# First modulation weights on ScalarE's queue, a fixed order of the first loads, new planning costs and new seeds in an attention-plus-MLP block

## The chip, the cores and the metric

The kernel runs on one core of one Trainium2 chip. The metric is the device time of one execution in microseconds (us), the median of three runs. Durations of single instructions come from one profiled execution.

## What is computed

One transformer block with adaptive layer norm, batch 1, 2048 positions, width 512, 32 heads of 16, hidden width 1376, all in bf16:

```python
mod = (_silu(c) @ w_mod).reshape(c.shape[0], 6, 1, -1)
sa, ca, ga, sb, cb, gb = (mod[:, 0], ..., mod[:, 5])
h = _layernorm(x) * (1 + ca) + sa
x = x + ga * _A_ref(h, A_wqkv, A_wo)         # attention: softmax(q k^T / 4) v, then @ wo
h = _layernorm(x) * (1 + cb) + sb
x = x + gb * _B_ref(h, B_w1, B_b1, B_w2, B_b2)   # gelu(h @ w1 + b1) @ w2 + b2
```

## The kernel before, in words

**Runs and tiles.** The 2048 positions form four blocks of 512 queries. A run is one block of queries with four heads; there are 32 runs, each over 16 tiles of 128 keys. One tile of one run is four score matrices of 128x512, one per head, called units here: 32 x 16 x 4 = 2048 units in all. TensorE multiplies the scores (L853), four heads at a time on four row groups of the array.

**Two engines make the exponentials.** ScalarE takes most units: TensorE writes three or two of them into one of two PSUM tiles `st` (three and two banks wide, in turn), and one ACTIVATE (L926) makes `pt` of them. The other units go to VectorE: TensorE writes one into a PSUM bank `ax`, VectorE turns it into an integer phase `ph` (L967), and then, once for four units, makes shifted copies `sh` (L987), four per tile, of which some fourth copies are made by GpSimd in four pieces `sg` (L1003). Reinterpreted as bf16, each copy is a coarse exponential, and the four together, weighted in the values `VX`, give a fine one. TensorE multiplies the results with the values into `od` (L1038). So an ScalarE tile costs one set of products, a VectorE tile four.

**What sets the order.** Every instruction stream is written out by hand from a planner (`Plan`) that runs while the program is built. It keeps a list of ready operations per engine, each with a planned duration and a priority; it commits the earliest, and breaks near ties with a pseudo-random term (`spread`) drawn from `SEEDS`, one seed for each 16 us of planned time. Planned durations decide which unit goes to which engine and where on TensorE's stream each product stands: `A_US` for ScalarE's ACTIVATEs of one, two or three units, `POOL_US` and `G_US` for GpSimd's pieces, `kb` for a load's landing (planned bytes over a planned rate). The engines then run these fixed streams; only semaphores decide the real times. Where the planner sees too little recent work on TensorE, it puts in filler products with a tile of zeros (`warm`): L463 and L468 before the first run, L479 (`zeros`, four products on `od`) beside a product set later.

**The start.** SyncE's queue issues, in this order: the first block of `x` in two halves (`xb`, L534), the first two 512-column parts of `w_mod` (1 MB into `g`, L544), the first 128 columns of the three projection weights (`w`, L551), the second block of `x` (L524), the other columns of the weights. ScalarE's queue issues `c` alone (L518). The modulation vectors are 32 narrow products with `g` (L611), copied by VectorE (L624, L625). The normalised block `z` is turned by TensorE (L687, 16 products), then scaled and shifted by the modulation on VectorE (L654, two quarters) and ScalarE (L651, two quarters) into `blk`; from `blk` come the first keys and queries (L730), and then the first scores.

**Late work.** After the first run, the remaining weights are loaded, some behind memsets on GpSimd that zero their padding (L1151 to L1153); after run 24 the last rows of `wo` are spread over a tile `wop` behind a memset (L1178). In each block's MLP a memset puts a row of ones into `g` (L1232), which brings in the bias. An operation of kind "beside" on GpSimd is planned beside a VectorE instruction, and waits for the VectorE instruction before that one (`after_dve`). After the last run come its division, the projection, the layer norm and the MLP of the last 256 positions, on TensorE almost without a break.

Of the kernel before, what the change touches and what calls it, by code (L numbers as in the profile page):

```python
# [11 lines left out]
ACT = mybir.ActivationFunctionType  # L12
# [51 lines left out]
FILL = 2.1  # L64
HOLD = 0.0
SPREAD = 0.15
SEEDS = (29, 932, 256, 388, 841, 336, 949, 269, 862, 134, 634, 182, 632, 486, 660, 374, 610, 152, 531, 667, 387, 332, 696, 744, 409, 494, 133, 981, 473, 660, 675, 515, 555, 629, 58, 269, 671, 382, 338, 452, 367, 48, 574, 712, 716, 126, 732, 265, 528, 970)
HEAT = 1.7


# [211 lines left out]
def kernel(  # L282
# [14 lines left out]
    nc = tc.nc  # L297
# [18 lines left out]
    FEW = 1  # L316
    MM = 0.2155
    SPAN = (3, 2)
    POOL_US, POOL_MIN = 0.68, 0.5
    G_US, G_MIN, G_PRIO, G_MAX, G_FROM, G_TILES = 0.70, 0.5, 1.0, 4, 60.0, 6  # L320
    A_US = {1: 0.477, 2: 0.904, 3: 1.3305}
    AHEAD = 3
    FIRST_DKS, D_TIME = (14,), 8.0

# [208 lines left out]
    for h in range(2):  # L533
        o_x0 += 2 * [dma(lambda o, h=h: nc.sync.dma_start(out=o_x[0].tile[:, 2 * h:2 * h + 2, :],  # L534
                                                         in_=x_src[0][:, 2 * h:2 * h + 2, :]),
                         (o_x[0],), kb=256, prio=0.0)]
    g0 = op("NIL", None, 0.0, (), lat=0.0, prio=-2.0, acq=r_g)

    def mod_pair(tile_):
# [1 line left out]

    def mod_part(tile_, n):
        return mod_pair(tile_)[:, :, n * D:(n + 1) * D]
    o_wm = dma(lambda o: nc.sync.dma_start(out=mod_pair(g0.tile), in_=wm_src[:, :, 0:2 * D]), (g0,), kb=1024, prio=0.01)  # L544
    o_w, o_w0 = {}, {}
    for i in range(3):
        o_w[i] = op("NIL", None, 0.0, (), lat=0.0, prio=-1.0 + 0.1 * i, acq=r_w)
# [1 line left out]
    def load_cols(i, lo, hi, prio):  # L549
        def go(o):  # L550
            nc.sync.dma_start(out=o_w[i].tile[:, :, lo:hi], in_=wq_src[:, :, i * D + lo:i * D + hi])  # L551
        return dma(go, (o_w[i],), kb=(hi - lo) * (2 if lo == 0 else 1), prio=prio, n=2.7)
    o_w0 = {i: load_cols(i, 0, P, 0.1 + 0.01 * i) for i in range(3)}
    o_w1 = {}
    for b in range(1, NQ):
        o_x[b] = load_x(b)
        o_x[b].prio = 0.2 + 0.1 * b
        o_w1[b - 1] = load_cols((1, 2, 0)[b - 1], P, D, 0.25 + 0.1 * b)
    o_w1 = {i: o_w1[(1, 2, 0).index(i)] for i in range(3)}

    o_id = op("POOL", lambda o: make_identity(nc, ident), 0.5, prio=0.0)
# [499 lines left out]
    def normalise(r):  # L1061
        last, od = o_last[r], o_od[r]
        OD = op("DVE", lambda o: nc.vector.tensor_copy(out=o.tile, in_=od.tile), 0.6, (last,),  # L1063
                prio=0.0, acq=r_OD, rel=(od,))
        st = {}

        def d1(o):
            st["dn"] = drp.tile([4, QB], FP32, name="dn")
            nc.sync.dma_start(out=st["dn"], in_=OD.tile[16:P:32, :])
        o1 = dma(d1, (OD,), kb=8, prio=0.0)  # L1070
        o2 = dma(lambda o: nc.sync.dma_start(
            out=o.tile, in_=st["dn"].rearrange("i (s e) -> (i s) e", e=16)), (o1,), kb=8, prio=0.0,
            acq=r_dc)
# [16 lines left out]
        two = beside(lambda c: nc.gpsimd.tensor_tensor(  # L1090
            out=OT.tile[:, c], in0=OD.tile[:, c], in1=o5.tile[:, c], op=ALU.mult), (OT,), (OD, o5), free=r == NR - 2)
        if not move:
            OT.two = two
            o_OT[(b, u // 2)] = OT
            return
        to = OT if b == LAST else o_OT[(b, u // 2)]

        def shift(o):
            for i in range(4):
                nc.sync.dma_start(out=to.tile[32 * i + 16:32 * i + 32, 0:HB] if b == LAST else  # L1100
                                  to.tile[32 * i + 16:32 * i + 32, :],
                                  in_=OT.tile[32 * i:32 * i + 16, HB:QB] if b == LAST else
                                  OT.tile[32 * i:32 * i + 16, :])
# [14 lines left out]
        return scaled([lambda f=f: W2[f // 4].tile[:, f % 4, :] if f < 8 else W2c[:, f - 8, :] for f in range(NF)],  # L1118
                      gb_bc, (W2[0], W2[1], o_late["small"], o_late["gb"]))

    def beside(fn, deps, rel=(), prio=0.5, free=False):

        if free:
            return [op("POOL", lambda o, c=c: fn(slice(c * HB, (c + 1) * HB)), POOL_US, deps, lat=0.1, prio=0.1,
                       rel=rel, port=True) for c in range(2)]
        return [op("POOL", lambda o, c=c: after_dve(fn(slice(c * HB, (c + 1) * HB))), POOL_US, deps, lat=0.1,
                   prio=prio, kind="beside", rel=rel, port=True, gate=lambda: plan.beside(POOL_MIN))
                for c in range(2)]

# [10 lines left out]
    def late_loads(after):  # L1140
# [7 lines left out]
        def wo(o):  # L1148
# [1 line left out]
        o_late["wo"] = dma(wo, d, kb=512)  # L1150
        z2 = op("POOL", lambda o: (nc.gpsimd.memset(W1[:, :, F:NF * P], 0.0),  # L1151
                                   nc.gpsimd.memset(b1_bf, 0.0),
                                   nc.gpsimd.memset(W2c[:, 2, :], 0.0)), 1.5, d, prio=8.0)  # L1153
        o_late["w1"] = dma(lambda o: nc.sync.dma_start(
            out=W1[:, :, 0:F], in_=B_w1.rearrange("(j p) n -> p j n", p=P)), (z2,), kb=1400)

# [13 lines left out]
    def split_wo():  # L1170
        held["wop"] = wop = op("NIL", None, 0.0, (), lat=0.0, prio=0.0, acq=r_w)

        def load(o):
            wo_src = A_wo[(NC - 1) * P:NC * P, :].rearrange("(r p d) f -> r p d f", r=4, p=2)
            for r in range(4):
                for p in range(2):
                    nc.sync.dma_start(out=wop.tile[32 * r:32 * r + 16, p, :], in_=wo_src[r, p])
        z1 = op("POOL", lambda o: nc.gpsimd.memset(wop.tile[:, 0:2, :], 0.0), 0.9, (wop,), prio=1.0)  # L1178
        ld = dma(load, (z1,), kb=128, n=8, prio=3.0)
        o_late["wop"] = scaled([lambda p=p: wop.tile[:, p, :] for p in range(2)], ga_bc, (ld,))  # L1180

    def fold_w1():
# [46 lines left out]
        return P if f < NF - 1 else FL  # L1229

    def ones(g, deps):
        return op("POOL", lambda o: nc.gpsimd.memset(g.tile[FL:P, NF - 1, :], 1.0), 0.4, deps, prio=0.0)  # L1232

    def finished():
        return units[0] == NR * NT * 4
# [317 lines left out]
```

## Time and profile before

| what | value |
|---|---|
| median of 3 runs (lowest to highest) | 775.24 us (774.72 to 776.56) |
| the profiled execution's own time | 774.01 us |
| span of its trace | 772.1 us |
| TensorE, VectorE, ScalarE, GpSimd busy | 94%, 93%, 96%, 43% of the span |
| granted TensorE clock | 0.998 |

A group of instructions is told by line, engine, operation, output and input tile; a busy time counts overlapping instructions once, a mean is that of single instructions. In the timeline a row gives the start, the length of a merged stretch of equal instructions, and their number; a bracket names the idle time ahead of it and what ended that. Consecutive instructions of one engine overlap, so their distance from start to start is shorter than their duration.

### The profile page before, as it was taken

The page shows a single profiled execution, that of the slowest core. Times are in us where ns is not written, and L with a number is a line of the kernel's source. Part 1 is how long each engine was busy: PE and PEld are TensorE (multiplying, and loading weights), DVE is VectorE, ACT ScalarE, POOL GpSimd, SP SyncE. Part 2 cuts the span into 40 slices and gives each one's busy share as a digit, 9 for nine tenths or more (in the row PEclk, how much of TensorE's full clock was granted, in tenths as well). Part 3 has the DMA queues.
Part 4 walks back from the last instruction along what each step waited for, and adds up shares of the span by engine and source line. Part 5 has one row for each costly group of instructions (what it writes and reads, how often), then busy time and mean ns, then how long its engine had stood idle before and what let it go on. Part 6 is the DMA issues. An engine that isn't in the chain of part 4 may idle for free. (4 is left out here: it accounts for less than half of the span.)

```text
span 772.1 us, 20489 instructions
## 1 busy us (share of the span) xinstructions
PE 726.5 (94%) x8066; PEld 263.9 (34%) x8066; DVE 718.5 (93%) x1233; ACT 744.8 (96%) x673; POOL 333.9 (43%) x604
## 2 busy tenths in 40 slices
PE   9999999999999989989999999999999899999997
PEld 4433333333332322222322222222233334433445
DVE  6889799889999999999999999999989999999984
ACT  4999999999999999999999999999999999999993
POOL 6512533555554454545541353434434544341441
PEclk9999999999999999999999999999999999999999
DMA  6151010100011001011110120001111111101100
GB/s 219 34 156 64 18 51 17 26 3 19 24 53 44 23 25 45 20 31 25 44 30 26 31 35 20 22 21 28 33 47 27 29 32 33 46 19 31 33 18 28
DMA packets 42162, 29.53 MB, mean 38 GB/s; under 512 B 25525, under 2 KB 35286, under 8 KB 42066
## 3 DMA queue, kind: packets, MB, share of 16 engines
q1 hardware_dynamic: 42058, 28.22, 13.1%
q8 instruction: 63, 1.03, 0.6%
q14 instruction: 33, 0.27, 0.1%
q10 hardware_dynamic: 8, 0.00, 0.0%
HBM read 20.77 MB, written 2.61 MB: 30 GB/s over the span
## 5 line engine op out<-in xcount | busy, mean ns | idle before, releaser
L926 ACT ACTIVATE pt<-st 128x1536 bf16<-128x1536 f32 (+1 forms) x621 | 704.4, 1350 | 3.7 <-PE ax L853 2.3
L967 DVE TENSOR_SCALAR ph<-ax 128x512 int16<-128x512 f32 x496 | 325.1, 681 | 23.1 <-PE ax L853 20.6
L1003 POOL TENSOR_SCALAR sg<-ph 128x512 int16<-128x512 int16 x320 | 199.8, 624 | 293.3 <-DVE sh L987 186.5
L987 DVE TENSOR_SCALAR sh<-ph 128x2048 int16<-128x2048 int16 x416 | 285.0, 715 | 1.9 <-PE od L1038 1.0
L853 PE MATMUL st<-qm,kT 32*128 32x512 bf16 x1552 | 243.2, 382 | 31.9 <-ACT pt L926 25.6
L853 PE MATMUL ax<-qm,kT 32*128 32x512 bf16 x496 | 170.4, 380 | 3.7 <-DVE ph L967 2.2
L853 PEld LDWEIGHTS <-kT 32*128 32x128 bf16 x2048 | 85.6, 91 | 250.1 <-issue 240.7
L1038 PE MATMUL od<-pt,VEB 128*32 128x512 bf16 (+1 forms) x1936 | 142.3, 341 | 1.5 <-DVE OD L1063 1.0
L1038 PE MATMUL od<-sh,VX 128*32 128x512 bf16 (+1 forms) x1464 | 110.5, 342 | 1.1 <-DVE sh L987 0.7
L1038 PEld LDWEIGHTS <-VEB 128*32 128x32 bf16 x2560 | 61.6, 96 | 75.1 <-issue 60.7
L1038 PEld LDWEIGHTS <-VX 128*32 128x32 bf16 x1872 | 44.4, 95 | 70.5 <-issue 63.3
L1038 PE MATMUL od<-sh,VEB 128*32 128x512 bf16 (+1 forms) x624 | 49.5, 341 | 0.3 <-DVE sh L987 0.2
L1090 POOL TENSOR_TENSOR OT<-OD,RB 128x256 bf16<-128x256 f32 x38 | 27.9, 745 | 43.5 <-DVE sh L987 33.6
L1284 PE MATMUL ax<-blk,W 128*128 128x512 bf16 (+1 forms) x176 | 43.6, 355 | 0.4 <-DVE ph L967 0.4
L479 PE MATMUL od<-warm 128*32 128x512 bf16 x416 | 40.4, 387 | 0.0
L730 PE MATMUL ax<-blk,w 128*128 128x512 bf16 x124 | 35.9, 382 | 0.5 <-ACT blk L651 0.2
L1225 PE MATMUL ax<-w,g 128*128 128x512 bf16 x128 | 34.4, 381 | 0.9 <-ACT g L1294 0.6
L1038 PE MATMUL od<-sg,VX 128*32 128x512 bf16 (+1 forms) x408 | 32.1, 338 | 0.2 <-POOL sg L1003 0.2
L788 POOL TENSOR_SCALAR VX<-VEB 128x128 bf16<-128x128 bf16 x60 | 22.4, 377 | 19.3 <-PE od L1038 10.7
L1289 DVE TENSOR_SCALAR g<-ax,b1c 128x512 bf16<-128x512 f32 (+1 forms) x44 | 29.2, 675 | 1.2 <-PE ax L1284 0.9
L1090 POOL TENSOR_TENSOR OS<-OD,RB 128x256 bf16<-128x256 f32 x24 | 17.1, 728 | 28.0 <-DVE sh L987 27.6
L635 DVE BATCH_NORM_STATS2 ln_s<-xb 128x6 f32<-128x512 bf16 x32 | 21.7, 677 | 1.4 <-DMA xb<-in_A_x_dram 1.4
(107 smaller groups left out, 412.1 us busy)
## 6 DMA issues: line engine op xcount, KB each, us to landing
RB<-rn SPq DMA_DIRECT2D x124, 64.0 KB
xb<-in_A_x_dram SPq DMA_DIRECT2D x7, 512.0 KB
g<-in_w_mod_dram SPq DMA_DIRECT2D x2, 1024.0 KB
out_dram<-o SPq DMA_DIRECT2D x16, 128.0 KB
qm<-qs SPq DMA_DIRECT2D x120, 16.0 KB
W<-in_B_w_dram SPq DMA_DIRECT2D x1, 1376.0 KB
w<-in_A_wqkv_dram SPq DMA_DIRECT2D x3, 384.0 KB
xb<-in_w_mod_dram SPq DMA_DIRECT2D x2, 512.0 KB
```

The costliest lines, as they stand in the source:

```text
L479: nc.tensor.matmul(out=o_od[r].tile[32 * i:32 * i + 32, :], lhsT=warm[:, 0:32], rhs=warm[:, 0:1].to_broadcast([P, QB]), start=False, stop= ...
L730: return chain([(lambda ps, j=j: nc.tensor.matmul(out=ps[:, 0:QB], lhsT=w.tile[:, j, cc * P:(cc + 1) * P], rhs=o_h[b].tile[:, j, :], start ...
L853: nc.tensor.matmul(out=o.tile[:, k * QB:(k + 1) * QB], lhsT=kT[cc][kb][rows, ko * P:(ko + 1) * P], rhs=qm.tile[rows, par, :] if hb is None ...
L926: nc.scalar.activation(out=e.tile[:, 0:total * QB], in_=o.tile[:, 0:total * QB], func=ACT.Exp, scale=ESC)
L967: nc.vector.tensor_scalar(out=ph.tile[:, o.row * QB:(o.row + 1) * QB], in0=o.tile, scalar1=PH_B, scalar2=PH_LOW, op0=ALU.add, op1=ALU.max)
L987: nc.vector.tensor_scalar(out=o.tile, in0=first.tile, scalar1=1.0 / FINE, scalar2=PH_0 + PH_SH[j], op0=ALU.mult, op1=ALU.add)
L1003: after_dve(nc.gpsimd.tensor_scalar(out=sh.tile[:, c], in0=first.tile[:, c], scalar1=1.0 / FINE, scalar2=PH_0 + PH_SH[j], op0=ALU.mult, op ...
L1038: nc.tensor.matmul(out=o_od[r].tile[32 * i:32 * i + 32, n * HB:n * HB + w], lhsT=v_tile(kt, ph)[:, c0:c0 + 32], rhs=got[i][:, at:at + w], ...
L1090: two = beside(lambda c: nc.gpsimd.tensor_tensor(out=OT.tile[:, c], in0=OD.tile[:, c], in1=o5.tile[:, c], op=ALU.mult), (OT,), (OD, o5), f ...
L1225: nc.tensor.matmul(out=ps, lhsT=g[:, f, col:col + P], rhs=rhs, start=(f == 0), stop=(f == NF - 1))
L1284: mm = chain([(lambda ps, f=f, j=j, f0=f0: nc.tensor.matmul(out=ps[:, (f - f0) * N:(f - f0 + 1) * N], lhsT=W1[:, j, f * P:(f + 1) * P], rh ...
L1289: ev.append(op("DVE", lambda o, f=f, f0=f0, mm=mm: nc.vector.tensor_scalar(out=g.tile[:, f, 0:N], in0=mm.tile[:, (f - f0) * N:(f - f0 + 1) ...
```

## The change

1. The 1 MB load of the first modulation weights is issued from ScalarE's queue, right behind the load of `c`; its planned size goes from 1024 to 1300 (kB), and the planner makes it depend on the load of `c`.
2. The first loads on SyncE's queue get priorities that fix their order: the halves of `x`, then the first columns of the weights in the order keys, queries, values (before: queries, keys, values), then in turn a block of `x` and the rest of one weight. The planned size of the first columns is halved.
3. Planned durations: ScalarE's ACTIVATEs from 0.477, 0.904, 1.3305 us to 0.487, 0.916, 1.344 us; GpSimd's multiplication of the attention output from 0.68 to 0.74 us; the late memsets from 1.5 to 1.2 and from 0.4 to 0.52 us, with the port that GpSimd shares with VectorE taken into account.
4. The memset of `wop` is cut into four pieces placed "beside" VectorE; the memset of ones is placed so too.
5. All 50 seeds are new.

```diff
-SEEDS = (29, 932, 256, ...)
+SEEDS = (432, 324, 180, ...)
...
-    POOL_US, POOL_MIN = 0.68, 0.5
+    POOL_US, POOL_MIN, N_US = 0.68, 0.5, 0.74
-    A_US = {1: 0.477, 2: 0.904, 3: 1.3305}
+    A_US = {1: 0.487, 2: 0.916, 3: 1.344}
...
-                         (o_x[0],), kb=256, prio=0.0)]
+                         (o_x[0],), kb=256, prio=-9.0 + h)]
...
-    o_wm = dma(lambda o: nc.sync.dma_start(out=mod_pair(g0.tile), in_=wm_src[:, :, 0:2 * D]), (g0,), kb=1024, prio=0.01)
+    o_wm = dma(lambda o: nc.scalar.dma_start(out=mod_pair(g0.tile), in_=wm_src[:, :, 0:2 * D]), (g0, o_c), kb=1300,
+               eng="ACT", prio=-7.0)
...
-        return dma(go, (o_w[i],), kb=(hi - lo) * (2 if lo == 0 else 1), prio=prio, n=2.7)
-    o_w0 = {i: load_cols(i, 0, P, 0.1 + 0.01 * i) for i in range(3)}
+        return dma(go, (o_w[i],), kb=hi - lo, prio=prio, n=2.7)
+    o_w0 = {i: load_cols(i, 0, P, -6.0 + (1, 0, 2)[i]) for i in range(3)}
...
-        o_x[b].prio = 0.2 + 0.1 * b
-        o_w1[b - 1] = load_cols((1, 2, 0)[b - 1], P, D, 0.25 + 0.1 * b)
+        o_x[b].prio = b - 3.5
+        o_w1[b - 1] = load_cols((1, 2, 0)[b - 1], P, D, b - 3.0)
...
-                                   nc.gpsimd.memset(W2c[:, 2, :], 0.0)), 1.5, d, prio=8.0)
+                                   nc.gpsimd.memset(W2c[:, 2, :], 0.0)), 1.2, d, prio=8.0, port=True)
...
-        z1 = op("POOL", lambda o: nc.gpsimd.memset(wop.tile[:, 0:2, :], 0.0), 0.9, (wop,), prio=1.0)
-        ld = dma(load, (z1,), kb=128, n=8, prio=3.0)
+        z1 = [x for p in range(2) for x in beside(
+            lambda c, p=p: nc.gpsimd.memset(wop.tile[:, p, c], 0.0), (wop,), us=0.35)]
+        ld = dma(load, z1, kb=128, n=8, prio=3.0)
...
-        return op("POOL", lambda o: nc.gpsimd.memset(g.tile[FL:P, NF - 1, :], 1.0), 0.4, deps, prio=0.0)
+        return op("POOL", lambda o: after_dve(nc.gpsimd.memset(g.tile[FL:P, NF - 1, :], 1.0)), 0.52, deps, lat=0.1, prio=0.0,
+                  kind="beside", port=True, gate=lambda: plan.beside(POOL_MIN))
```

Since the planner lays out every stream anew, the instruction lists of the two built programs differ beyond these lines. Counted in the two lists:

| instructions | before | after |
|---|---|---|
| ScalarE, ACTIVATE of three units / of two units | 310 / 311 | 310 / 309 |
| VectorE, `ph` / `sh` | 496 / 416 | 500 / 421 |
| GpSimd, `sg` pieces | 320 | 316 |
| TensorE, products with the values, in sets of four | 660 whole, 448 half-width | 663 whole, 448 half-width |
| TensorE, filler sets of four on `od` (L479, and L1029 at a run's start) | 104 + 8 | 121 + 8 |
| TensorE, fillers of full width (L463, L468) | 51 | 47 |
| TensorE, ahead of the narrow products of L611: fillers / products that turn `z` | 29 / 0 | 30 / 8 |

In the lists of the changed kernel the last streams, from the last score product to the end, hold the same instructions as before in a slightly different order.

More of the change, by code (lines that the diff above doesn't have):

```diff
@@ L66 @@
 SPREAD = 0.15
-SEEDS = (29, 932, 256, 388, 841, 336, 949, 269, 862, 134, 634, 182, 632, 486, 660, 374, 610, 152, 531, 667, 387, 332, 696, 744, 409, 494, 133, 981, 473, 660, 675, 515, 555, 629, 58, 269, 671, 382, 338, 452, 367, 48, 574, 712, 716, 126, 732, 265, 528, 970)
+SEEDS = (432, 324, 180, 701, 660, 159, 105, 688, 614, 64, 722, 921, 341, 292, 667, 446, 7, 423, 524, 376, 479, 681, 179, 178, 891, 61, 111, 982, 774, 605, 458, 798, 627, 354, 348, 796, 559, 345, 786, 415, 117, 962, 210, 627, 701, 917, 778, 631, 597, 949)
 HEAT = 1.7
@@ L1090, in normalise @@
         two = beside(lambda c: nc.gpsimd.tensor_tensor(
-            out=OT.tile[:, c], in0=OD.tile[:, c], in1=o5.tile[:, c], op=ALU.mult), (OT,), (OD, o5), free=r == NR - 2)
+            out=OT.tile[:, c], in0=OD.tile[:, c], in1=o5.tile[:, c], op=ALU.mult), (OT,), (OD, o5), free=r == NR - 2, us=N_US)
         if not move:
@@ L1119, in w2_scaled, with beside @@
                       gb_bc, (W2[0], W2[1], o_late["small"], o_late["gb"]))
-    def beside(fn, deps, rel=(), prio=0.5, free=False):
+    def beside(fn, deps, rel=(), prio=0.5, free=False, us=POOL_US):
         if free:
-            return [op("POOL", lambda o, c=c: fn(slice(c * HB, (c + 1) * HB)), POOL_US, deps, lat=0.1, prio=0.1,
+            return [op("POOL", lambda o, c=c: fn(slice(c * HB, (c + 1) * HB)), us, deps, lat=0.1, prio=0.1,
                        rel=rel, port=True) for c in range(2)]
-        return [op("POOL", lambda o, c=c: after_dve(fn(slice(c * HB, (c + 1) * HB))), POOL_US, deps, lat=0.1,
+        return [op("POOL", lambda o, c=c: after_dve(fn(slice(c * HB, (c + 1) * HB))), us, deps, lat=0.1,
                    prio=prio, kind="beside", rel=rel, port=True, gate=lambda: plan.beside(POOL_MIN))
```

## The prediction

> **What bounds the kernel now.** I read the page's busy times first, then the windows by stage, then who waited for whom, then the groups by form.
>
> ```profile
> PE 726.5 (94%) x8066; PEld 263.9 (34%) x8066; DVE 718.5 (93%) x1233; ACT 744.8 (96%) x673; POOL 333.9 (43%) x604
> ```
> ```profile
> 200.00:300.00 100.00, 92.83 (x1000) 29.88 (x998) 98.38 (x161) 100.00 (x89) 49.13 (x82) 1.00 0.12 35
> 300.00:400.00 100.00, 93.52 (x901) 29.26 (x898) 98.91 (x167) 99.70 (x86) 49.87 (x78) 1.00 0.11 29
> 751.00:772.10 21.10, 17.24 (x150) 10.34 (x148) 9.61 (x24) 9.15 (x28) 2.12 (x5) 1.00 0.08 26
> ```
> ```profile
> ACT pt L926 <- PE ax L853: 2.3, 4, 0.9
> ACT pt L926 <- PE st L853: 0.9, 2, 0.5
> PE st L853 <- ACT pt L926: 25.6, 88, 0.8
> DVE ph L967 <- PE ax L853: 20.6, 38, 2.5
> ```
> ```profile
> 15.28 6.88 ACT L926 ACTIVATE pt<-st 128x1536 bf16<-128x1536 f32 x6 [0.38 <-PE st L853]
> 749.62 1.28 ACT L1294 ACT_TABLE_LOAD   x1
> ```
>
> The columns of the window rows after the length are TensorE, its weight loads, VectorE, ScalarE and GpSimd busy. Three engines look alike on the page; the windows and waits part them. In the middle ScalarE is busy 100.00 and 99.70 of 100 us. It waited visibly for score products only 2.3 + 0.9 us in the whole run, while TensorE waited 25.6 us, 88 times, for ScalarE to free a score tile, and VectorE then 20.6 us for TensorE. So ScalarE sets the pace from its first exponential at 15.28 us to the end of its last at 749.62. What comes behind (22.5 us) is TensorE's. The span thus has three terms: the start, ScalarE's stream, the tail.
>
> How full is that stream really? Neighbouring ACTIVATEs overlap, so a late one can hide in the busy time.
>
> ```profile
> 493.83 24.96 ACT L926 ACTIVATE pt<-st 128x1024 bf16<-128x1024 f32 x22
> 517.09 1.71 ACT L926 ACTIVATE pt<-st 128x1536 bf16<-128x1536 f32 x1
> L926 ACT ACTIVATE pt<-st 128x1536 bf16<-128x1536 f32 x310 | 484.2, 1562 | 2.4 <-PE ax L853 1.1 <-PE st L853 0.9 <-ACT pt L926 0.2
> L926 ACT ACTIVATE pt<-st 128x1024 bf16<-128x1024 f32 x311 | 353.9, 1139 | 1.3 <-PE ax L853 1.2
> L926 ACT ACTIVATE pt<-st 128x1536 bf16<-128x1536 f32 (+1 forms) x621 | 704.4, 1350 | 3.7 <-PE ax L853 2.3
> ```
>
> The first two rows are a stretch without idle time: the last of its 22 starts at 517.09, so 21 distances take 23.26 us, two-unit ones 11 times and three-unit ones 10 times in turn. A third unit costs 1.562 - 1.139 = 0.423 us. Hence 21a + 10 x 0.423 = 23.26: a = 0.906 us for two units, 1.329 for three. At that pace the 621 would take 310 x 1.329 + 311 x 0.906 = 693.8 us; they took 704.4. ScalarE is thus late by 10.6 us in all, most of it hidden. I call this its lateness; it is the term on which the forecast hangs.
>
> **The change part by part.**
>
> *The split of the units.* The changed program has two two-unit ACTIVATEs fewer: 2 x 0.906 = 1.8 us off the bounding stream. VectorE gets four `ph` and five `sh` more.
>
> ```profile
> L967 DVE TENSOR_SCALAR ph<-ax 128x512 int16<-128x512 f32 x496 | 325.1, 681 | 23.1 <-PE ax L853 20.6
> L987 DVE TENSOR_SCALAR sh<-ph 128x2048 int16<-128x2048 int16 x416 | 285.0, 715 | 1.9 <-PE od L1038 1.0
> ```
>
> By their busy shares that is 4 x 325.1/496 + 5 x 285.0/416 = 6.0 us, spread over 735 us, in an engine that has 23.1 us of idle time ahead of `ph` alone. GpSimd has four pieces fewer. TensorE has three product sets more, and 17 filler sets (121 for 104). I count the 1.8 us as gained, and the rest as covered by VectorE's waits for TensorE; without that cover, at most 6.0 us would show.
>
> *The new planned pace.* The plan now takes 0.916 and 1.344 us where the stretch above ran at 0.906 and 1.329: over the stream it lays TensorE's work out for a ScalarE that is 310 x 0.015 + 309 x 0.010 = 7.7 us slower than it can be. If TensorE kept exactly to the plan, ScalarE would be late by those 7.7 us instead of 10.6, a gain of 2.9 us. Local slips come on top: the 17 fillers are product time on TensorE's own stream, and one filler takes what the next rows show.
>
> ```profile
> 52.01 0.39 PE L479 MATMUL od<-warm 128*32 128x512 bf16 x4
> 52.23 0.39 PE L1038 MATMUL od<-pt,VEB 128*32 128x512 bf16 x3
> 53.52 0.39 PE L853 MATMUL st<-qm,kT 32*128 32x512 bf16 x2
> 54.01 2.37 ACT L926 ACTIVATE pt<-st 128x1024 bf16<-128x1024 f32 x2 [0.35 <-PE ax L853]
> ```
>
> A filler starts at 52.01, the next set at 52.23: 0.22 us. A little later the scores come late and ScalarE idles 0.35 us. All 17 on the path would be 17 x 0.22 = 3.7 us of new lateness. So this term lies between -2.9 and +3.7 us. The old row, 10.6 us, is nearest to both, and I take it unchanged: 0.
>
> *The start.*
>
> ```profile
> 0.72 0.54 ACTq L518 DMA_DIRECT2D c_bf<-in_c_dram  x1
> 1.64 0.43 SPq L544 DMA_DIRECT2D g<-in_w_mod_dram  x1
> 2.59 0.31 ACT L594 ACTIVATE ce<-c_bf 4x128 f32<-4x128 bf16 x1
> 3.99 0.54 POOL L598 TENSOR_SCALAR ce<-ce 4x128 f32<-4x128 f32 x1
> 3.94 1.49 PE L463 MATMUL ax<-warm 128*128 128x512 bf16 x3
> 9.37 0.60 PE L463 MATMUL ax<-warm 128*128 128x512 bf16 x2
> 9.81 0.87 PEld L611 LDWEIGHTS <-g 128*128 128x128 bf16 x32 [0.34 <-DMA g<-in_w_mod_dram]
> 10.61 0.90 PEld L687 LDWEIGHTS <-z 128*128 128x128 bf16 x16
> 11.01 0.26 DVE L625 TENSOR_SCALAR modA<-modA 128x4 f32<-128x4 f32 x1
> 11.50 0.99 DVE L654 TENSOR_SCALAR blk<-st,modA 128x512 bf16<-128x512 bf16 x2 [0.23 <-PE st L687]
> 11.72 1.45 ACT L651 ACTIVATE blk<-st,modA 128x512 bf16<-128x512 bf16 x2 [4.04 <-PE st L687]
> 12.78 0.69 DVE L635 BATCH_NORM_STATS2 ln_s<-xb 128x6 f32<-128x512 bf16 x1 [0.28 <-DMA xb<-in_A_x_dram]
> ```
>
> The load of `g` would be issued at about 1.26 (end of the issue of `c`) instead of 1.64; its issue of 0.43 us stands ahead of ScalarE's table load and pushes `ce` from 2.59 + 0.31 = 2.90 to about 3.3, still ahead of GpSimd's use at 3.99. The three small weight loads behind it on SyncE's queue are issued 0.43 us sooner, keys first. But does `g` bind? The last two fillers start at 9.37 and 0.22 later, so TensorE is done with them at 9.81, just when the narrow products begin: load and fillers end together. In the changed list 30 fillers and 8 products turning `z` stand ahead of them, for 29 and 0. That is 0.22 + 8 x 0.90/16 = 0.67 us more on a stream without a gap. However early `g` lands, L611's work starts at 10.48. The modulation is ready 11.27 - 9.81 = 1.46 us later, at 11.94, and the second half of the turning is done by then. ScalarE's quarters, which waited for that turning until 11.72, then start at 12.0: the earlier turning gives back part of the 0.67. The first keys and the first scores wait for the second of these quarters, so the first exponential comes 0.3 us later. From below: with 0.67 us less on TensorE the quarters could start right at 11.27, 0.45 us sooner.
>
> These fillers are also where a rule bears. At 3.94 three of them take 0.43 us each (to the next rows' 0.22), so TensorE starts slow. The Trainium skill, "TensorE: Matmul & The Clock Gate", Part 1, says the array runs at half rate for about 3.4 us of work, and that the number of slow products differs from run to run. Here the halving agrees (0.43 to 0.22); that it varies no run here shows. By that rule the start could fall on either side of my 0.3 us.
>
> *Memsets.*
>
> ```profile
> L1178 POOL MEMSET w<- 128x1024 bf16 x1 | 1.0, 958 | 0.1
> 752.41 0.61 PE L1364 MATMUL t<-w,OT 128*128 128x512 bf16 x2
> ```
>
> Four pieces of about 0.958/4 = 0.24 us each take the place of 0.96 us; each waits for a VectorE instruction, up to 0.7 us (the means of `ph` and `sh`), with GpSimd's pieces `sg` queued behind it. The tile is needed at 752.41 only, and GpSimd is busy 43%: nothing on the path. The memset of ones likewise waits for VectorE, behind it `sg` pieces, and in the tail the layer norm's scale; there the instruction it waits for ends before ScalarE's activation that it waits for anyway. Bounds 0 to 0.7 us, taken as 0.
>
> *The tail* holds the same instructions; TensorE's stream after 751 is 17.24 of 21.10 us: 0.
>
> Sum: -1.8 + 0 + 0.3 + 0 = -1.5 us, on the profiled execution's own 774.01 us (span 772.1 and 1.9 around it): 772.5. The median stands 1.23 above that execution, so I forecast 773.7.
>
> **The rivals.** About 0.2% (1.55 us) is what a measurement here can tell from no change, so the line to "faster" is 773.7 too; the forecast lies on it.
>
> *Lateness up (slower).* Place: TensorE's stream ahead of the score products. The 17 fillers and VectorE's 6.0 us more work, in windows where it is busy 98 to 99%, make scores late oftener. Price with all fillers on the path: -1.5 + 3.7 = +2.2, so 777.4. It is slower from 3.05 us of added lateness on, 29% of the 10.6. For it: a filler stands shortly ahead of the late scores at 53.52. Against: TensorE waits 25.6 us for ScalarE, so most of its slips are absorbed.
>
> *Lateness down (faster).* The plan's slower ScalarE fits the real one, TensorE stalls less and VectorE starves less: -1.5 - 2.9 = -4.4, so 770.8; with a start that gains 0.45 instead of losing 0.3, 770.1.
>
> *The load lands later, so the change doesn't do what it says.* On its own queue `g` is no longer ahead of the loads behind it.
>
> ```profile
> DMA packets 1587, 1.70 MB, mean 212 GB/s; under 512 B 856, under 2 KB 856, under 8 KB 1587
> ```
>
> In this row of the first 8 us, 856 small packets, those of the weights issued behind `g`, had moved before `g` was in: even one queue mixed them. At worst `g` lands with the second block of `x`, which VectorE awaited until 12.78: L611 moves from 10.48 to 12.78, 2.3 us, and the total is -1.5 + 2.3 = +0.8, so 776.0. The Trainium skill, "DMA: Bandwidth & Descriptors", section "Issuing engines are not separate DMA queues", says that such DMAs interleave on the same 16 engines whoever issued them; that speaks against a gain, and the trace agrees as far as the 856 packets go.
>
> **How the numbers follow.** Forecast 0.42 (own range 772.4 to 775.0, half on each side of the line: 0.21 faster, 0.21 same). Lateness up 0.27, nearly all slower. Lateness down 0.22, faster. Late load 0.09, mostly same. Together: faster 0.43, same 0.29, slower 0.28. The range takes in both bounds of the lateness, the start's gain and a late load beside more lateness: 769.0 to 778.5.
>
> **What would show it.** The ACTIVATE group should fall to x619 and about 702.6 us busy; its excess over 693.8 - 1.8 = 692.0 us is the lateness (10.6 expected, 7.7 or 14.3 by the rivals). L611's weights should start near 10.5 without waiting for `g`, and the first exponential near 15.6. From the last exponential to the end 22.5 us should remain. I am wrong if the first exponential moves by over 1 us, if VectorE or TensorE rather than ScalarE is full in the middle, or if the lateness leaves 7.7 to 14.3.

## The result, and the profile after

| | before | after |
|---|---|---|
| median of 22 runs each (lowest to highest) | 774.69 us (772.94 to 776.56) | 771.91 us (771.02 to 775.16) |
| the profiled execution's own time | 774.01 us | 771.48 us |
| its span | 772.1 us | 769.5 us |
| start, up to the first exponential | 15.28 us | 14.83 us |
| ScalarE's stream, up to the table load behind its last exponential | 734.34 us | 732.13 us |
| tail | 22.48 us | 22.54 us |

The change makes the kernel faster by a little: the ratio is 0.9969, with a 95% interval of 0.9961 to 0.9977, which is 2.4 us (1.8 to 3.0); the medians of the table are 2.8 us apart. In the two profiles 2.2 us of it come out of ScalarE's stream and 0.45 us out of the start.

The lines below answer to those of before in the prediction. First the page's busy times:

```profile
PE 731.3 (95%) x8142; PEld 262.7 (34%) x8142; DVE 720.6 (94%) x1242; ACT 742.9 (97%) x671; POOL 330.8 (43%) x603
```

The windows of the middle and of the tail (length, then TensorE, its weight loads, VectorE, ScalarE, GpSimd busy, granted clock, DMA share, GB/s):

```profile
200.00:300.00 100.00, 95.34 (x1032) 30.25 (x1035) 99.59 (x166) 100.00 (x90) 43.07 (x69) 1.00 0.13 34
300.00:400.00 100.00, 94.83 (x965) 28.17 (x958) 99.30 (x169) 99.96 (x90) 48.23 (x76) 1.00 0.11 29
748.40:769.50 21.10, 17.52 (x150) 10.35 (x149) 9.98 (x24) 9.08 (x28) 2.12 (x5) 0.98 0.08 26
```

Who waited for whom (in total, times, longest):

```profile
ACT pt L927 <- PE ax L854: 2.0, 2, 1.6
ACT pt L927 <- PE st L854: 0.9, 2, 0.5
PE st L854 <- ACT pt L927: 17.4, 60, 0.8
DVE ph L968 <- PE ax L854: 16.0, 24, 2.8
```

The groups of the exponentials and of VectorE's `ph`:

```profile
L927 ACT ACTIVATE pt<-st 128x1536 bf16<-128x1536 f32 x619 | 702.5, 1343 | 3.3 <-PE ax L854 2.0
L968 DVE TENSOR_SCALAR ph<-ax 128x512 int16<-128x512 f32 x500 | 327.2, 681 | 18.2 <-PE ax L854 16.0
```

ScalarE is still the full engine (100.00 and 99.96 of 100 us), and still waits visibly for scores only 2.0 + 0.9 us. What filled up are the other two: VectorE is busy 99.59 of 100 us where it was 98.38, TensorE 95.34 where it was 92.83, and both wait less for others (17.4 for 25.6 us, 16.0 for 20.6 us). The group of exponentials has two instructions fewer and is 704.4 - 702.5 = 1.9 us shorter; its visible idle time went from 3.7 to 3.3 us. Together with 0.1 us more in ScalarE's other work this is the stream's 2.2 us. The lateness, as the prediction measures it, is 702.5 - 692.0 = 10.5 us, where it was 10.6.

The start, from the timeline of the changed kernel:

```profile
1.30 0.42 ACTq L544 DMA_DIRECT2D g<-in_w_mod_dram  x1
3.04 0.31 ACT L595 ACTIVATE ce<-c_bf 4x128 f32<-4x128 bf16 x1
3.94 0.73 PE L463 MATMUL ax<-warm 128*128 128x512 bf16 x2
4.51 0.38 PE L468 MATMUL od<-warm 128*128 128x512 bf16 x1
4.72 0.60 PE L463 MATMUL ax<-warm 128*128 128x512 bf16 x2
9.52 1.06 PEld L612 LDWEIGHTS <-g 128*128 128x128 bf16 x32
9.73 0.94 PE L612 MATMUL ax<-sc,g 128*128 128x1 bf16 x32
11.18 1.45 ACT L652 ACTIVATE blk<-st,modA 128x512 bf16<-128x512 bf16 x2 [3.80 <-PE st L688]
14.83 2.37 ACT L927 ACTIVATE pt<-st 128x1536 bf16<-128x1536 f32 x2 [0.38 <-PE st L854]
746.96 1.28 ACT L1297 ACT_TABLE_LOAD   x1
```

The load of `g` is issued at 1.30 and `ce` is done at 3.35, both as forecast; by its semaphore `g` is in at 7.84 us, where it came at 9.77. The narrow products nevertheless start at 9.73, without waiting for it: TensorE works on fillers and turning products without a break until then. In this trace the fillers come 0.22 us apart from about 4.5 us on; before, three at 3.94 were still 0.43 apart, and by the trace's record of the clock the array had its full rate from 5.7 us on, here from 4.2 (until then a filler takes 0.43 us). That is why the start is 0.45 us shorter and not 0.3 longer.

### The profile page after: what moved, and what is told of

Its sections match the earlier page's. It is cut to its first block, busy times and chain, and to the rows that moved or that the text cites. A ratio compares the mean times of both kernels' runs of the same rounds, so it can differ in the third digit from the quotient of the medians.

```text
span 769.5 us, 20634 instructions
## 1 busy us (share of the span) xinstructions
PE 731.3 (95%) x8142; PEld 262.7 (34%) x8142; DVE 720.6 (94%) x1242; ACT 742.9 (97%) x671; POOL 330.8 (43%) x603
## 5 line engine op out<-in xcount | busy, mean ns | idle before, releaser
L927 ACT ACTIVATE pt<-st 128x1536 bf16<-128x1536 f32 x619 | 702.5, 1343 | 3.3 <-PE ax L854 2.0
L1004 POOL TENSOR_SCALAR sg<-ph 128x512 int16<-128x512 int16 x316 | 196.4, 622 | 262.9 <-DVE sh L988 186.2
L854 PE MATMUL st<-qm,kT 32*128 32x512 bf16 x1548 | 242.3, 383 | 21.3 <-ACT pt L927 17.4
L854 PE MATMUL ax<-qm,kT 32*128 32x512 bf16 x500 | 174.0, 379 | 3.1 <-DVE ph L968 1.8
L854 PEld LDWEIGHTS <-kT 32*128 32x128 bf16 x2048 | 79.8, 91 | 241.0 <-issue 232.3
L1039 PE MATMUL od<-pt,VEB 128*32 128x512 bf16 (+1 forms) x1932 | 139.7, 340 | 0.6 <-DVE OD L1064 0.5
L479 PE MATMUL od<-warm 128*32 128x512 bf16 x484 | 46.2, 388 | 0.0
L789 POOL TENSOR_SCALAR VX<-VEB 128x128 bf16<-128x128 bf16 x60 | 20.7, 347 | 30.9 <-DVE VEB L662 27.6
```

Source lines behind the costliest of these rows:

```text
L479: nc.tensor.matmul(out=o_od[r].tile[32 * i:32 * i + 32, :], lhsT=warm[:, 0:32], rhs=warm[:, 0:1].to_broadcast([P, QB]), start=False, stop= ...
L854: nc.tensor.matmul(out=o.tile[:, k * QB:(k + 1) * QB], lhsT=kT[cc][kb][rows, ko * P:(ko + 1) * P], rhs=qm.tile[rows, par, :] if hb is None ...
L927: nc.scalar.activation(out=e.tile[:, 0:total * QB], in_=o.tile[:, 0:total * QB], func=ACT.Exp, scale=ESC)
L1004: after_dve(nc.gpsimd.tensor_scalar(out=sh.tile[:, c], in0=first.tile[:, c], scalar1=1.0 / FINE, scalar2=PH_0 + PH_SH[j], op0=ALU.mult, op ...
L1039: nc.tensor.matmul(out=o_od[r].tile[32 * i:32 * i + 32, n * HB:n * HB + w], lhsT=v_tile(kt, ph)[:, c0:c0 + 32], rhs=got[i][:, at:at + w], ...
```

## The experiments

All times are medians; ratios are to the kernel before, run beside them on the same chip. "Full rate from" is the time at which the trace's record of the clock first shows full speed.

### Is it the load? e1 and e9

e1 is the kernel before with nothing but the queue of this load changed.

```diff
-    o_wm = dma(lambda o: nc.sync.dma_start(out=mod_pair(g0.tile), in_=wm_src[:, :, 0:2 * D]), (g0,), kb=1024, prio=0.01)
+    o_wm = dma(lambda o: nc.scalar.dma_start(out=mod_pair(g0.tile), in_=wm_src[:, :, 0:2 * D]), (g0,), kb=1024, prio=0.01)
```

> The kernel before, with the load of g issued on ScalarE's queue and nothing else moved: the plan and every other stream stay as they were. Theory A (the gain is ScalarE's two pieces fewer; the start is set by TensorE's fillers, not by g): g lands about 2 us sooner, near 7.8 us, but 29 fillers still stand ahead of the narrow products, which start at 9.8 us if TensorE quickens at 5.9 us as before, and about 0.7 us sooner if it quickens at 4.5 as in the profile after; the time stays within 0.1% of before. Theory B (the load's queue brought the gain): the first exponential moves from 15.28 to 14.8 us whatever the fillers do, and the time falls by 0.5 us or more.

Measured: 773.70 us against 774.88, ratio 0.9991 (0.9980 to 1.0001): not told from no change. Its timeline, the window of a later stretch and its group:

```profile
8.59 1.06 PEld L611 LDWEIGHTS <-g 128*128 128x128 bf16 x32
14.26 2.37 ACT L926 ACTIVATE pt<-st 128x1536 bf16<-128x1536 f32 x2 [0.38 <-PE st L853]
```
```profile
160.70:167.50 6.80, 6.80 (x61) 1.86 (x64) 4.45 (x9) 4.96 (x5) 2.23 (x4) 0.50 0.02 2
```
```profile
L926 ACT ACTIVATE pt<-st 128x1536 bf16<-128x1536 f32 (+1 forms) x621 | 704.6, 1365 | 4.9 <-PE ax L853 3.6
```

`g` was in at 7.97, and with the array at full rate from 3.7 us the first exponential came at 14.26, 1.02 us sooner than in the profile of before. But the end of the stream is no sooner (750.01 for 749.62): from 160.7 to 167.5 us TensorE ran at half clock, for 6.8 us, where before had 3.4 (162.7 to 166.1), and ScalarE's visible idle time rose from 3.7 to 4.9 us. So the move can gain something in the kernel before, where in its one profile `g` at 9.77 us is a floor for the start. By the ratio it is 0.7 us with an interval that touches none; among runs with the same granted clock it is 1.1 to 1.2 us (table in the next section).

e9 is the changed kernel with the load put back on SyncE's queue; it is the counter-test. The plan's cost for it and the order of the other loads stay.

```diff
-    o_wm = dma(lambda o: nc.scalar.dma_start(
+    o_wm = dma(lambda o: nc.sync.dma_start(
```

> The changed kernel with the load of g issued on SyncE's queue again (behind the halves of x and the first weights of the keys), every other stream unchanged. Theory D (the narrow products start at the later of two things, TensorE done with fillers and turning, and g landed): g lands near 9.8 us instead of 7.8 to 8.5; if TensorE reaches full rate near 4 us, g binds and the first exponential comes up to 0.5 us later than in the changed kernel; if it does near 7 us, fillers bind and nothing changes. Time 0 to 0.5 us above the changed kernel. If the queue carried the gain: 1 us or more above.

Measured: 772.64 us, ratio 0.9976 (0.9966 to 0.9985); the changed kernel itself, run again beside it as e12, had 772.88 and 0.9974 (0.9963 to 0.9985). By the ratios there is no difference.

```profile
2.12 0.51 SPq L544 DMA_DIRECT2D g<-in_w_mod_dram  x1
10.47 1.07 PEld L612 LDWEIGHTS <-g 128*128 128x128 bf16 x32
15.79 1.45 ACT L927 ACTIVATE pt<-st 128x1536 bf16<-128x1536 f32 x1 [0.38 <-PE st L854]
```

The load is issued 0.82 us later than in the changed kernel's first profile and lands 0.86 us later (8.70 for 7.84, where 9.8 was expected), and TensorE is again not ready for it. The narrow products are later than in the first profile because the array came to full rate at 6.1 us here. So the start of the changed kernel doesn't hang on the queue of this load. Among runs with the same granted clock, e9 is still about 0.5 us slower than the changed kernel, on seven runs, and its profile's stream is 0.6 us longer; whether the other loads on SyncE's queue, issued later now, have to do with that wasn't tried.

### What lies ahead of the load? e3, e4, e11

The same edit with three bounds: of the 30 fillers at the start (L463, L468), the last 3, 10 or 16 are not issued. Only products with a tile of zeros are left out. For e3:

```diff
-            return Op("PE", lambda o: nc.tensor.matmul(
+            return Op("PE", lambda o: n_heat.append(1) if 27 <= len(n_heat) < 30 else n_heat.append(nc.tensor.matmul(
...
```

with 20 in place of 27 for e4, and 14 for e11.

> The changed kernel without the three fillers that stand between the first turning of z and the narrow products; the other instructions keep their order. If fillers set the start (A): the narrow products and the first exponential come 3 x 0.22 = 0.65 us sooner than in the changed kernel in the same run, and the time is 0.65 us lower, 0.08%. If g or z sets it (B): no change.

> The changed kernel without the ten fillers from the transposition of c to the narrow products. Theory A: the narrow products then wait for g (7.8 us) and z instead, and start near 8.1 us; the second block's statistics, which stand ahead of the queries' copies on VectorE and wait for its load (11.6 us), become the next thing that is late; first exponential 1.1 us sooner than in the changed kernel, time lower by 1.1 us. If TensorE falls back to the slow rate in the gap, each product until it recovers costs 0.2 us more and the gain is lost. Theory B: no change.

> The changed kernel without fillers 15 to 30 of the start; the other instructions in the same order. With ten fewer the first exponential was at 14.0 us although TensorE was slow until 7.0 us. Theory D: TensorE is then through with the 14 left by 7.0 us at the latest, c's transposition follows, and g (8.0 to 8.5 us) and z bind: narrow products near 8.3 us, first exponential near 13.6 us, time 1.2 to 1.5 us below the changed kernel. If fewer fillers put off the full rate beyond 7.0 us, the gain is lost.

Measured: e3 771.31 us, 0.9957 (0.9941 to 0.9973); e4 770.76, 0.9943 (0.9925 to 0.9961); e11 769.68, 0.9938 (0.9921 to 0.9956). The times of e3 and e4 can't be told from the changed kernel's beside them (e2 below, 0.9944 to 0.9973); their starts can be compared with each other. The timelines of e3, e4 and e11:

```profile
10.43 0.94 PE L612 MATMUL ax<-sc,g 128*128 128x1 bf16 x32
15.53 1.45 ACT L927 ACTIVATE pt<-st 128x1536 bf16<-128x1536 f32 x1 [0.38 <-PE st L854]
```
```profile
6.07 0.63 PE L468 MATMUL od<-warm 128*128 128x512 bf16 x1
6.50 0.84 PE L463 MATMUL ax<-warm 128*128 128x512 bf16 x2
7.17 0.38 PE L468 MATMUL od<-warm 128*128 128x512 bf16 x1
8.92 0.94 PE L612 MATMUL ax<-sc,g 128*128 128x1 bf16 x32
14.02 2.37 ACT L927 ACTIVATE pt<-st 128x1536 bf16<-128x1536 f32 x2 [0.38 <-PE st L854]
```
```profile
7.30 0.88 PE L688 MATMUL st<-ident,z 128*128 128x128 bf16 x8 [1.20 <-DVE z L647]
8.13 0.86 PEld L612 LDWEIGHTS <-g 128*128 128x128 bf16 x32
13.41 3.71 ACT L927 ACTIVATE pt<-st 128x1536 bf16<-128x1536 f32 x3 [0.38 <-PE st L854]
744.12 1.28 ACT L1297 ACT_TABLE_LOAD   x1
```

e3 and e4 both had full rate only from 7.0 us on (e4's rows show the fillers 0.43 apart up to 6.5). So both missed the starts expected of them: e3's came later than the changed kernel's, and in e4 the fillers still bound, not `g` and `z`. Between them lie seven fillers, and the narrow products lie 10.43 - 8.92 = 1.51 us apart: 0.216 each, so every filler is on the path, as the prediction had it. e4's first exponential is 0.81 us before that of the changed kernel's first profile, and its last ends at 746.16, 0.80 sooner: what the start gains reaches the end. In e11 the chain changes over: its 14 fillers are done early, TensorE idles 1.20 us until the first of `z` is there, and the narrow products start at 8.13, behind the turning and right when `g` lands (8.09). Here at last `z` and the load bind, within about 0.1 us of each other, so dropping still more fillers should bring the start nothing. e11 is the fastest version, faster than the kernel before and than the changed one beside it (its interval and e12's don't overlap). Of its profile's 2.8 us against the first profile of the changed kernel (744.12 for 746.96) 1.42 lie in the start; the other 1.4 us are told of with the half-clock stretches below.

### The changed kernel itself, again: e2 and e12

Both are the changed kernel as it is: e2 was run beside e1, e3 and e4, e12 beside e9 to e11.

> The changed kernel once more, for a second look at its start. Theory A: the time is 0.997 of before again; the first exponential is at 14.8 us if the slow phase of TensorE ends near 4.5 us, and near 15.6 us if it ends near 5.9 us, since the number of fillers is fixed. Theory B: 14.8 us in either case.

> The changed kernel once more, on the same chip as the others of this job. 0.996 to 0.997 of before; first exponential 14.8 to 15.5 us by the time at which TensorE gets its full rate; one slow stretch of TensorE of 3.4 or 6.8 us between 130 and 170 us, which costs ScalarE's stream about as much as before.

Measured: e2 771.65 us, 0.9959 (0.9944 to 0.9973); e12 772.88, 0.9974 (0.9963 to 0.9985), with two slow stretches of 3.4 us where one was expected. Their timelines, e2 first:

```profile
9.69 1.06 PEld L612 LDWEIGHTS <-g 128*128 128x128 bf16 x32
15.18 1.45 ACT L927 ACTIVATE pt<-st 128x1536 bf16<-128x1536 f32 x1 [0.38 <-PE st L854]
```
```profile
10.04 1.06 PEld L612 LDWEIGHTS <-g 128*128 128x128 bf16 x32
15.43 1.45 ACT L927 ACTIVATE pt<-st 128x1536 bf16<-128x1536 f32 x1 [0.38 <-PE st L854]
```

Three profiles of one program thus give three starts. Full rate came at 4.2, 4.6 and 5.3 us, and the narrow products at 9.73, 9.91 and 10.26: about half a microsecond for each microsecond, as it must be when a microsecond at half rate does half the fillers. Carried on to the 5.7 us of the profile of before, they would start at 10.45; 5.10 us behind that, as in the first profile, the first exponential would come at about 15.55.

### The memsets: e10

The changed kernel with the first of the four pieces clearing all of `wop`'s two rows at once, and the memset of ones without its wait for VectorE.

```diff
-            lambda c, p=p: nc.gpsimd.memset(wop.tile[:, p, c], 0.0), (wop,), us=0.35)]
+            lambda c, p=p: nc.gpsimd.memset(wop.tile[:, 0:2, :] if (p, c.start) == (0, 0) else wop.tile[:, p, c], 0.0), (wop,), us=0.35)]
...
-        return op("POOL", lambda o: after_dve(nc.gpsimd.memset(g.tile[FL:P, NF - 1, :], 1.0)), 0.52, ...
+        return op("POOL", lambda o: (nc.gpsimd.memset(g.tile[FL:P, NF - 1, :], 1.0)), 0.52, ...
```

> The changed kernel with the first of the four pieces of the memset of wop clearing the whole tile (0.96 us; the three others still run) and the memsets of ones without their wait for VectorE. My step: they are covered, time within 0.5 us of the changed kernel, lateness unchanged. Rival: GpSimd's uncut piece holds the shared port against VectorE, scores come late, time up by about 1 us near the place of that memset.

Measured: 771.60 us, 0.9961 (0.9949 to 0.9973).

```profile
747.03 1.28 ACT L1297 ACT_TABLE_LOAD   x1
```

The last exponential ends 0.07 us from the changed kernel's. Pieces or whole, the memsets are worth nothing that shows.

### The later fillers: e8

The rival of more lateness put its price on the fillers in the stream. e8 takes away 80 of the sets beside the products (L479); only products with zeros are left out.

```diff
-            if o.extra:
+            if o.extra and False:
                 zeros(r)
```

> The changed kernel without 80 of its 121 filler sets on od (those beside a product set), the other instructions in the same order. If fillers make scores late (my slower rival): 80 x 0.22 = 17.6 us leave TensorE's stream and the lateness falls by up to 3.7 us. If they fill time in which TensorE would wait anyway (A): lateness and time within 1 us, unless the granted clock falls, in which case the time rises.

Measured: 775.33 us, 1.0019 (0.9995 to 1.0044): 3.4 us above the changed kernel's median. Windows of two of its slow stretches, then its group:

```profile
140.60:147.40 6.80, 6.75 (x72) 1.99 (x69) 4.85 (x9) 6.35 (x6) 2.62 (x4) 0.50 0.02 2
229.30:236.10 6.80, 6.73 (x50) 1.38 (x53) 5.89 (x11) 5.65 (x5) 3.41 (x6) 0.50 0.06 12
```
```profile
L927 ACT ACTIVATE pt<-st 128x1536 bf16<-128x1536 f32 x619 | 703.3, 1349 | 6.1 <-PE st L854 3.9
```

Without them TensorE ran at half clock for 23.8 us of the middle, in five stretches between 140 and 417 us, where the changed kernel has 3.4 us. The exponentials' busy time did not fall (703.3 for 702.5), and their visible idle time nearly doubled (6.1 for 3.3). That alone leaves open whether fewer fillers gained something which the half clock took away again. Laid side by side exponential by exponential, the two profiles show hardly any such gain: at 136.9 us, ahead of its first half-clock stretch and with 8 sets fewer, e8 has gained 0.02 us on the changed kernel since the first exponential. Behind its last stretch (417 us) it lags by 3.9 us and at the end by 3.5, with 22 sets fewer in between: 0.02 us a set, where the prediction priced 0.22. So these fillers are next to no price in the sum: they hold the clock, and TensorE's waits take them in.

### The plan: e5, e6, e7

What did the new seeds and the new costs do, each alone? e5 is the changed kernel with the seeds of before; e6 with a third set of seeds (the changed ones times 7 plus 123, modulo 1000); e7 with the old planned durations of the ACTIVATEs and the changed seeds.

```diff
-SEEDS = (432, 324, 180, ...)
+SEEDS = (29, 932, 256, ...)        # e5
+SEEDS = (147, 391, 383, ...)       # e6
...
-    A_US = {1: 0.487, 2: 0.916, 3: 1.344}
+    A_US = {1: 0.477, 2: 0.904, 3: 1.3305}     # e7
```

> The changed kernel with the 50 seeds of before. Its program has 313 three-unit, 312 two-unit and one one-unit ACTIVATEs, for 310 and 309. Theory A (the seeds matter through the number of units that the plan leaves to ScalarE): at 1.329 and 0.906 us (0.48 for the single one) its stream is 7.1 us longer than the changed kernel's, lateness stays near 10.5 us, time 7 us above the changed kernel, about 779. Theory C (the seeds matter through how late the score products come): the lateness moves by several us and the time does not follow the count. If seeds do nothing: 772.

> The changed kernel with a third, arbitrary set of 50 seeds (each new seed times 7 plus 123, modulo 1000). Its program has 311 three-unit, 311 two-unit and one one-unit ACTIVATEs. Theory A: stream 3.6 us longer than the changed kernel's, time about 775.5. Theory C: lateness moves instead, time not ordered by the count.

> The changed kernel with the planned ACTIVATE durations of before (0.477, 0.904, 1.3305 us). Its program has 314 and 313 ACTIVATEs. Theory A: stream 8.9 us longer, time about 781. A rival to it (a plan that takes ScalarE at its real pace keeps TensorE ahead): lateness falls by up to 3 us, time about 778.

Measured: e5 788.98 us, 1.0179 (1.0160 to 1.0198); e6 787.93, 1.0160 (1.0133 to 1.0188); e7 790.39, 1.0198 (1.0180 to 1.0216). All three expectations were too low by far; this is the largest miss of the study. The groups, and the ends of the streams, of e5, e6 and e7:

```profile
L927 ACT ACTIVATE pt<-st 128x1536 bf16<-128x1536 f32 x626 | 711.6, 1328 | 7.2 <-PE st L854 3.0
760.74 1.28 ACT L1297 ACT_TABLE_LOAD   x1
```
```profile
L927 ACT ACTIVATE pt<-st 128x1536 bf16<-128x1536 f32 x623 | 706.9, 1335 | 6.2 <-PE od L1039 2.7
755.05 1.28 ACT L1297 ACT_TABLE_LOAD   x1
```
```profile
L927 ACT ACTIVATE pt<-st 128x1536 bf16<-128x1536 f32 x627 | 712.5, 1354 | 10.1 <-PE od L1039 4.2
763.66 1.28 ACT L1297 ACT_TABLE_LOAD   x1
```

The prediction's own measure tells where the time went. Other seeds leave ScalarE more units: seven, four and eight exponentials more, which at full pace (0.906 and 1.329 us, and about half of 0.906 for a single unit) is 699.1, 695.6 and 700.9 us where the changed kernel has 692.0. The lateness is 711.6 - 699.1 = 12.5, then 11.3 and 11.6; the visible idle time is 7.2, 6.2 and 10.1 us for 3.3. And the tails are 787.5 - 760.74 = 26.8, 31.2 and 23.8 us for 22.5. For e5 these are 7.1 + 2.0 + 3.9 + 4.2 = 17.2 of the 18.0 us that the spans differ by, and 0.6 more is its later start. A part of this is the clock again: TensorE ran at half clock for 10.2 us in e5 (from 142.0), for 3.4 and 6.8 us in e6 (the 6.8 in its tail, from 759.7) and for 6.8 in e7, where the changed kernel has 3.4. But e6's one run at a granted clock of 0.997 still took 784.69 us. A plan is thus good for its seeds and its costs together; neither the old seeds with the new costs nor the new seeds with the old ones come near it, and a third set doesn't either.

## Why the prediction was right

**ScalarE sets the pace, and two of its instructions go.** Right. Predicted 1.8 us off the stream and x619 at about 702.6 us; measured 2.21 us and x619 at 702.5.

**The lateness stays.** Right in the value, 10.5 for 10.6, and on weaker ground than it looked. The prediction set a gain of 2.9 us from the slower planned pace against a price of 3.7 us for the fillers, and took 0 between them. e8 shows that the price was next to none, and e7 that the planned pace can't be judged apart: with the old costs the plan under the new seeds is 18 us worse. So the 10.5 belongs to this pair of seeds and costs, and that it lies so near the old value was luck, not a finding of the prediction. Had the change kept the old seeds (e5, 14.2 us slower than before), the count of the finished lists would have shown 699.1 - 693.8 = 5.3 us of that; a lateness taken as unchanged and a tail taken at nothing would have hidden the rest.

**VectorE's 6.0 us more are covered.** Right: it is fuller, its waits for TensorE fell from 20.6 to 16.0 us, and ScalarE's for scores did not rise.

**The start.** The step was right and its term mis-sized: "However early `g` lands, L611's work starts at 10.48" gave +0.3 us, and the profile shows -0.45. Fillers and turning do set it (e3, e4), `g` is hidden behind them (e9), and the give-back is there: from the narrow products to the first exponential it is 14.83 - 9.73 = 5.10 us, where before had 15.28 - 9.81 = 5.47, so 0.37 us as in the forecast (0.67 - 0.3). What failed is that 10.48 took over the profile of before's share of slow fillers. With full rate from 5.7 us it would have come out as predicted (10.45, from e2 and e12); the array warmed 1.5 us sooner. The rule that the prediction cited beside this, the Trainium skill's "TensorE: Matmul & The Clock Gate", Part 1, that the number of slow products differs from run to run, is borne out by these runs: full rate came at 4.2, 4.6 and 5.3 us in one program, at 3.7 to 7.0 over all. What it says of the length, half rate for about 3.4 us of work, holds only roughly: TensorE works from 0.98 us on, so here it was 2.7 to 6.0 us.

**The load.** The rival that it lands later is refuted: 7.84 us for 9.77, and 7.8 to 8.5 in all other profiles with it on ScalarE's queue. That its landing gains the start nothing is right for the changed kernel: until fillers were dropped (e11), its narrow products waited for the load in no profile, e9's included. For the kernel before it isn't: with the load moved, e1's weights of the narrow products start at 8.59 us, ahead of the 9.77 at which `g` had landed; that load and fillers ended together was the late full rate of one profile. The other rule cited, "DMA: Bandwidth & Descriptors" of the Trainium skill, section "Issuing engines are not separate DMA queues", grants a change of queue only the time of the issue. e9 fits that (issue 0.82 us later, landing 0.86 later); e1 does not: its load is issued at 1.29 for 1.64 and lands at 7.97 for 9.77, 0.35 us sooner in and 1.80 sooner out. There the measurement decides. The load's semaphore rises in 16 steps, and in the profile of before 13 of them had come by 8.04 us; the 1.80 us are in the last three (9.46, 9.56 and 9.77), and what held those wasn't tried.

**Memsets and tail.** Both 0, as predicted (e10; 22.54 for 22.48 us).

**The sum.** Forecast -1.5, measured -2.6 in the profiles: 0.75 us of the difference is the start, 0.4 the stream. In the medians the rest of the way from 773.7 to 771.91 is that the kernel before had 774.69 in these runs, 0.55 less than in its first three. The rival of more lateness fell with the measured 10.5 and with e8; that of less lateness would have shown 7.7 us of it, and the 10.5 rules it out, so the few tenths that the stream gained beyond 1.8 us are no sign of it.

**How much is the clock.** Every run has a granted clock, averaged over it. In these profiles 0.999 and more goes with no half-clock stretch in mid-stream, 0.997 or 0.998 with one of 3.4 us, and 0.995 or 0.996 with 6.8 us (next section). The medians in us, with the number of runs (before as it ran beside e1 to e12, without two runs at 0.993; the changed kernel with e2 and e12):

| granted clock | before | changed kernel | e1 | e9 | e11 |
|---|---|---|---|---|---|
| 0.999 to 1.000 | 772.90 (8) | 771.02 (5) | none | 772.58 (1) | 768.57 (2) |
| 0.997 to 0.998 | 774.19 (13) | 771.91 (24) | 773.05 (4) | 772.51 (5) | 769.68 (2) |
| 0.995 to 0.996 | 775.12 (26) | 773.74 (10) | 773.90 (7) | 774.19 (2) | 771.92 (2) |

In each row the changed kernel is 1.4 to 2.3 us faster than the kernel before, so the gain doesn't come from the clock alone. The rest of the difference is that the lowest row holds 26 of 47 runs of before and 10 of 39 of the changed kernel. **Open** is whether the change brought that about, and how much of each row's gain is the start, which the profiles show to differ by up to 1 us between runs of near-equal kernels.

## What to carry to other kernels

Before a load is moved forward, look at what its consumer's engine does just before it: here 1 MB came two microseconds sooner and the changed kernel's products were not ready for it, because a stream without a gap stood ahead; cutting that stream brought them 1.6 us forward (9.73 to 8.13). Measure the engine that bounds the kernel by its instructions times their distance in an undisturbed stretch, and call the rest its lateness; it shows in one number whether a new plan is better or only different. Where a plan has random seeds, parts of a change to its costs can't be tested one by one against it: an altered cost under seeds that belong to another plan lost 16 to 18 us here, many times what the part is worth. How the seeds of the two kernels were found isn't on record.

## What the runs showed of the hardware

TensorE fell to half clock in the middle of a dense stream, for 3.4 us or a multiple of it. Every profile but e11's has a stretch that begins between 138 and 163 us, with 20 to 32 narrow products of one column in the 4 us ahead of it (L1187 before, L1189 after). But e11 has these products and no stretch, and e12's second, one in e6, one in e7 and four of e8's five have none of them ahead; so what brings a stretch about isn't known. When one begins has a pattern that the trace's record of the clock shows: always a whole number of times 3.413 us behind the first full rate, 41 times in the changed kernel (139.95 us), 46 in the kernel before (157.01), 39 and 40 in e3 and e4. A shifted start thus changes which products fall between two such marks. The kernel before had this window:

```profile
162.70:166.10 3.40, 3.40 (x40) 0.93 (x28) 2.29 (x5) 2.97 (x3) 1.03 (x2) 0.50 0.01 2
```

The windows of the changed kernel around its stretch, and its ScalarE behind it:

```profile
140.00:144.10 4.10, 3.43 (x57) 1.58 (x49) 3.31 (x6) 4.10 (x5) 1.99 (x4) 1.00 0.03 6
144.10:147.50 3.40, 3.40 (x31) 0.88 (x28) 1.41 (x3) 2.10 (x2) 0.69 (x1) 0.51 0.03 2
147.50:151.00 3.50, 3.50 (x47) 0.89 (x43) 3.15 (x7) 3.20 (x4) 1.60 (x3) 0.99 0.03 2
```
```profile
147.80 2.37 ACT L927 ACTIVATE pt<-st 128x1024 bf16<-128x1024 f32 x2 [1.60 <-PE ax L854]
```

The array was busy 3.43 of the 4.10 us before, and still the next 3.4 us ran at 0.51: 31 products where the 3.5 us after it hold 47, and ScalarE idle for 1.60 us. e12 had two such stretches, and e11 none. These are e12's, and e11's window at the same place:

```profile
145.20:148.60 3.40, 3.40 (x36) 0.79 (x28) 1.92 (x3) 2.16 (x3) 0.69 (x1) 0.50 0.02 2
165.70:169.10 3.40, 3.40 (x26) 1.52 (x25) 1.51 (x3) 3.07 (x3) 1.63 (x4) 0.50 0.00 0
```
```profile
144.10:147.50 3.40, 3.40 (x51) 0.88 (x43) 3.20 (x7) 3.38 (x4) 1.89 (x3) 1.00 0.03 3
```

| profile | full rate from | first exponential | half clock in mid-stream | ScalarE's stream |
|---|---|---|---|---|
| before | 5.7 us | 15.28 us | 3.4 us | 734.3 us |
| e1 | 3.7 | 14.26 | 6.8 | 735.8 |
| after | 4.2 | 14.83 | 3.4 | 732.1 |
| e2 (after again) | 4.6 | 15.18 | 3.4 | 732.1 |
| e12 (after again) | 5.3 | 15.43 | 6.8 | 733.0 |
| e11 | 4.7 | 13.41 | none | 730.7 |

The last four rows have the same instructions behind the start. A stretch of 3.4 us costs ScalarE's stream 0.9 to 1.4 us there (0.7 in e3, 731.4 us, where it begins at 140.1 us), and whether it comes once, twice or not at all differs between runs. Half of e11's lead in its profile is of this kind. That is not the work of its fewer fillers alone: its six runs have granted clocks from 0.995 to 0.999, so the stretches come there too, and in each row of the table above it leads the changed kernel by 1.8 to 2.5 us.
